# Linear attention over 32 heads: sixteen single warm-up matmuls, a new order for the first heads, and stores spread among the loads

## The chip, the cores and the metric

The kernel runs on one core of one Trainium2 chip. The metric is device time in microseconds (us); lower is better. Five engines run their own instruction lists at the same time: TensorE (PE, matmuls, with PEld for its weight loads), VectorE (DVE), ScalarE (ACT), GpSimd (POOL) and SyncE (SP, which here only issues DMAs). Sixteen DMA engines move the data between memory (HBM) and the core's buffer.

## What is computed

For each of 32 heads, with sequence length S = 2048 and head size D = 128, all in bf16:

```python
phi_q = jnp.where(q > 0, q + 1, jnp.exp(q)) + 1e-6
phi_k = jnp.where(k > 0, k + 1, jnp.exp(k)) + 1e-6
kv = jnp.einsum("bhsd,bhse->bhde", phi_k, v)
z = jnp.einsum("bhsd->bhd", phi_k)
num = jnp.einsum("bhqd,bhde->bhqe", phi_q, kv)
den = jnp.einsum("bhqd,bhd->bhq", phi_q, z)[..., None] + 1e-6
return num / den
```

Each head reads q, k and v (512 KB each) and writes 512 KB. The kernel splits phi(x) into min(exp(x), 1) + 1e-6 and max(x, 0), keeps the two parts apart, and lets TensorE add their products.

## The kernel before

A head is one tile of 128 partitions by 16 blocks of 128 rows. The work of head h is a set of named operations, and every operation is added once in `head(h)`:

- `ldk`, `ldq`, `ldv` (L347): loads of 512 KB into one of NI = 7 buffers each. All are issued by SP, except `ldv0.0`, which ACT issues. A load of head h waits until head h - 7 has been read.
- `ek` (L360, ACT): exp of k; `em` (L363, DVE): min with 1 and add 1e-6, in place. `rkp` (L370, POOL) and, for the first half of head 0 only, `rkd` (L366, DVE): max(k, 0). `v1` (L374, POOL): a copy of v beside a column of ones (`v1ones`, L324). The results of `em`, `rkp` and `v1` have two buffers each, freed by `kv` of two heads before.
- `kv` (L381, PE): 32 matmuls of 129 columns into one PSUM bank that holds both kv and z. `kvs` (L386, DVE): its copy to bf16.
- `T` (L393, PE): 16 transposes of q into PSUM, one buffer only: `T` of the next head waits for `eq` (L397, ACT, exp), `rqa` (L403, ACT, relu of the first half) and `rqb` (L406, DVE, the same for the second half). `emq` (L399, DVE): min with 1 and add 1e-6.
- `n.0` and `n.1` (L417 to L424, PE): the product of phi(q) with kv, 129 columns, in two groups: blocks 0 to 11 in PSUM banks 0 to 3, blocks 12 to 15 in banks 4 and 5. Then on DVE `a` (L437, adds 1e-6 for the second group), `r` (L440, reciprocal) and `f` (L444, the product with the reciprocal, to one of NO = 12 output buffers). `a.1` of head h waits for `kv` of head h + 2, because they share bank 5.
- `st` (L452, SP): the store of a head, 512 KB; the last head is stored in three pieces.
- `w` (L326 to L335, PE): warm-up matmuls of 480 columns on the identity matrix, into a PSUM bank that is not yet in use. They wait for nothing but the identity matrix, so each runs when TensorE's list reaches it.

There is no planner in the kernel: the table `ORDER` (L96) writes out the order of operations on each of the five engines by hand, and every engine runs its list strictly in that order. `Program.resolve` (L194) puts a semaphore wait before an operation for what it needs from another engine. SP's list is one queue: a store that waits for its `f` holds up all loads behind it. `WARM` (L13) gives the number of matmuls in `w0`, `w1`, `w2`.

The loads of heads 1 to 31 are shaped so that memory is read in 32 rows of 16 KB; a store writes 128 rows of 4 KB. SP issues far ahead: a load lands about 18 us after its issue.

Of the kernel before, what the change touches and what calls it, by code (L numbers as in the profile page):

```python
# [94 lines left out]

ORDER = {  # L96
    "PE": """
        w2 w1 T0.0 T0.1 w0 T1.0 kv0.0 kv0.1 n0.0 kv1.0 T2.0 n0.1 kv2.0 n1.0 n1.1 T3.0 kv3.0 n2.0 T4.0 n2.1 kv4.0
        n3.0 T5.0 n3.1 kv5.0 n4.0 T6.0 n4.1 kv6.0 n5.0 T7.0 n5.1 kv7.0 n6.0 T8.0 n6.1 kv8.0 n7.0 T9.0 n7.1 kv9.0
        n8.0 T10.0 n8.1 kv10.0 n9.0 T11.0 n9.1 kv11.0 n10.0 T12.0 n10.1 kv12.0 n11.0 T13.0 n11.1 kv13.0 n12.0  # L100
        T14.0 n12.1 kv14.0 n13.0 T15.0 n13.1 kv15.0 n14.0 T16.0 n14.1 kv16.0 n15.0 T17.0 n15.1 kv17.0 n16.0
        T18.0 n16.1 kv18.0 n17.0 T19.0 n17.1 kv19.0 n18.0 T20.0 n18.1 kv20.0 n19.0 T21.0 n19.1 kv21.0 n20.0
        T22.0 n20.1 kv22.0 n21.0 T23.0 n21.1 kv23.0 n22.0 T24.0 n22.1 kv24.0 n23.0 T25.0 n23.1 kv25.0 n24.0
        T26.0 n24.1 kv26.0 n25.0 T27.0 n25.1 kv27.0 n26.0 T28.0 n26.1 kv28.0 n27.0 T29.0 n27.1 kv29.0 n28.0
        T30.0 n28.1 kv30.0 n29.0 T31.0 T31.1 n29.1 kv31.0 n30.0 n30.1 n31.0 n31.1 n31.2
    """,
    "DVE": """
        eps0 ones emq0.0 em0.0 em0.1 rqb0.0 rkd0.0 v1ones0 v1ones1 eps1 emq0.1 em1.0 eps2 kvs0 emq1.0 r0.0
        rqb1.0 em2.0 kvs1 f0.0 em3.0 a0.1 r0.1 kvs2 f0.1 rqb2.0 r1.0 f1.0 emq2.0 em4.0 a1.1 r1.1 rqb3.0 f1.1
        r2.0 kvs3 f2.0 emq3.0 em5.0 a2.1 r2.1 rqb4.0 f2.1 r3.0 kvs4 f3.0 emq4.0 em6.0 a3.1 r3.1 rqb5.0 f3.1 r4.0  # L110
        kvs5 f4.0 emq5.0 em7.0 a4.1 r4.1 rqb6.0 f4.1 r5.0 kvs6 f5.0 emq6.0 em8.0 a5.1 r5.1 rqb7.0 f5.1 r6.0 kvs7
        f6.0 emq7.0 em9.0 a6.1 r6.1 rqb8.0 f6.1 r7.0 kvs8 f7.0 emq8.0 em10.0 a7.1 r7.1 rqb9.0 f7.1 r8.0 kvs9
        f8.0 emq9.0 em11.0 a8.1 r8.1 rqb10.0 f8.1 r9.0 kvs10 f9.0 emq10.0 em12.0 a9.1 r9.1 rqb11.0 f9.1 r10.0
        kvs11 f10.0 emq11.0 em13.0 a10.1 r10.1 rqb12.0 f10.1 r11.0 kvs12 f11.0 emq12.0 em14.0 a11.1 r11.1
        rqb13.0 f11.1 r12.0 kvs13 f12.0 emq13.0 em15.0 a12.1 r12.1 rqb14.0 f12.1 r13.0 kvs14 f13.0 emq14.0
        em16.0 a13.1 r13.1 rqb15.0 f13.1 r14.0 kvs15 f14.0 emq15.0 em17.0 a14.1 r14.1 rqb16.0 f14.1 r15.0 kvs16
        f15.0 emq16.0 em18.0 a15.1 r15.1 rqb17.0 f15.1 r16.0 kvs17 f16.0 emq17.0 em19.0 a16.1 r16.1 rqb18.0
        f16.1 r17.0 kvs18 f17.0 emq18.0 em20.0 a17.1 r17.1 rqb19.0 f17.1 r18.0 kvs19 f18.0 emq19.0 em21.0 a18.1
        r18.1 rqb20.0 f18.1 r19.0 kvs20 f19.0 emq20.0 em22.0 a19.1 r19.1 rqb21.0 f19.1 r20.0 kvs21 f20.0 emq21.0
        em23.0 a20.1 r20.1 rqb22.0 f20.1 r21.0 kvs22 f21.0 emq22.0 em24.0 a21.1 rqb23.0 r21.1 f21.1 r22.0 kvs23  # L120
        f22.0 emq23.0 em25.0 a22.1 r22.1 rqb24.0 f22.1 r23.0 kvs24 f23.0 emq24.0 em26.0 a23.1 r23.1 rqb25.0
        f23.1 r24.0 kvs25 f24.0 emq25.0 em27.0 a24.1 r24.1 rqb26.0 f24.1 r25.0 kvs26 f25.0 emq26.0 em28.0 a25.1
        r25.1 rqb27.0 f25.1 r26.0 kvs27 f26.0 emq27.0 em29.0 a26.1 r26.1 rqb28.0 f26.1 r27.0 kvs28 f27.0 emq28.0
        em30.0 a27.1 r27.1 rqb29.0 f27.1 kvs29 r28.0 emq29.0 f28.0 em31.0 a28.1 kvs30 rqb30.0 r28.1 f28.1 r29.0
        emq30.0 f29.0 emq31.0 emq31.1 a29.1 r29.1 kvs31 f29.1 emq31.2 r30.0 f30.0 a30.1 r30.1 f30.1 r31.0 f31.0
        a31.1 r31.1 r31.2 f31.1 f31.2
    """,
    "ACT": """
        exp ldv0.0 ek0.0 ek0.1 eq0.0 eq0.1 rqa0 ek1.0 eq1.0 ek2.0 rqa1 ek3.0 eq2.0 rqa2 ek4.0 eq3.0 rqa3 ek5.0
        eq4.0 rqa4 ek6.0 eq5.0 rqa5 ek7.0 eq6.0 rqa6 ek8.0 eq7.0 rqa7 ek9.0 eq8.0 rqa8 ek10.0 eq9.0 rqa9 ek11.0  # L130
        eq10.0 rqa10 ek12.0 eq11.0 rqa11 ek13.0 eq12.0 rqa12 ek14.0 eq13.0 rqa13 ek15.0 eq14.0 rqa14 ek16.0
        eq15.0 rqa15 ek17.0 eq16.0 rqa16 ek18.0 eq17.0 rqa17 ek19.0 eq18.0 rqa18 ek20.0 eq19.0 rqa19 ek21.0
# [6 lines left out]
        rkp6.0 v17.0 rkp7.0 rkp8.0 v18.0 rkp9.0 v19.0 rkp10.0 v110.0 v111.0 rkp11.0 v112.0 rkp12.0 v113.0
        rkp13.0 v114.0 rkp14.0 v115.0 rkp15.0 v116.0 rkp16.0 rkp17.0 v117.0 rkp18.0 v118.0 v119.0 rkp19.0 v120.0  # L140
        rkp20.0 rkp21.0 v121.0 rkp22.0 v122.0 rkp23.0 v123.0 rkp24.0 v124.0 rkp25.0 v125.0 v126.0 rkp26.0 v127.0
        rkp27.0 v128.0 rkp28.0 v129.0 rkp29.0 v130.0 rkp30.0 rkp31.0 v131.0
# [355 lines left out]
```

## Time and profile before

| what | value |
|---|---|
| time, median of 3 runs | 169.61 us (169.48 to 169.76) |
| the profiled execution's own time | 170.02 us |
| its span, first to last instruction | 168.6 us |
| busy: PE, DVE, ACT, POOL | 155.6, 153.7, 149.6, 93.4 us |
| moved by DMA | 67.51 MB, mean 400 GB/s over the span |
| HBM read, written | 50.33 MB, 16.78 MB |
| one head on PE in the middle of the run | 4.62 us |
| share of PE in the chain that ended last | 88% |

The profile is of one execution. Times are counted from the start of its span; the execution takes 1.4 us more than the span (170.02 against 168.6). A row of instructions gives when it began, how long it took, and in brackets how long its engine had been idle and what ended that. A row of a window gives, for each engine, how long it was busy in the window, then the granted TensorE clock (1.00 is full), the share of the 16 DMA engines that was busy (it can be a little over 1, since packets overlap) and the rate at which they moved data. A DMA issue has the time of the issue and the time from there to landing, when the last byte has arrived and the semaphore counts it.

### The profile page before, as it was taken

How to read it: one execution, taken by the hardware profiler on the slowest of the kernel's cores; microseconds unless marked ns; L12 is line 12 of the kernel's file. 1: busy time of each engine (PE TensorE's matmuls, PEld its weight loads, DVE VectorE, ACT ScalarE, POOL GpSimd, SP SyncE). 2: the span in 40 equal slices, each digit the busy share in tenths (PEclk: the TensorE clock that was granted, in tenths of full speed). 3: DMA queues.
4: the chain of work that ended last, by engine and by line, in shares of the span. 5: the costliest groups of instructions: out<-in, count | busy, mean ns of one | idle time of the engine just before them, and what ended most of it. 6: DMA issues, size and time to landing. Idle time of an engine off the chain costs nothing.

```text
span 168.6 us, 6160 instructions
## 1 busy us (share of the span) xinstructions
PE 155.6 (92%) x2702; PEld 151.2 (90%) x2702; DVE 153.7 (91%) x300; ACT 149.6 (89%) x102; POOL 93.4 (55%) x71
## 2 busy tenths in 40 slices
...
DMA  5999999999999999999999999999999999999985
GB/s 206 431 420 424 385 431 393 412 412 406 416 400 412 408 404 408 390 436 402 395 429 419 408 421 425 417 389 430 433 406 404 412 445 390 420 417 414 391 326 225
DMA packets 9819, 67.51 MB, mean 400 GB/s; under 512 B 2080, under 2 KB 2464, under 8 KB 6816
## 3 DMA queue, kind: packets, MB, share of 16 engines
...
q8 instruction: 21, 0.34, 0.8%
...
HBM read 50.33 MB, written 16.78 MB: 398 GB/s over the span
## 4 chain that ended last, share of the span: by engine, by line
PE 88%; DVE 6%; DMA 3%; ACT 1%; issue 0%; SPq 0%
PE la L381 35%; PE la L422 18%; PE la L393 17%; PE la L424 17%; DMA la<-in_q_dram 3%; DVE la L444 3%; DVE la L399 1%; DVE la L363 1%; ACT la L397 1%; DVE la L440 1%; PE la L417 0%; DVE la L406 0%; SPq L348 0%; DVE la L386 0%; DVE la L437 0%
## 5 line engine op out<-in xcount | busy, mean ns | idle before, releaser
L444 DVE TENSOR_TENSOR la<-la 128x1536 bf16<-128x1536 f32 (+2 forms) x65 | 77.7, 1197 | 0.2
L370 POOL TENSOR_SCALAR la<-la 128x2048 bf16<-128x2048 bf16 (+1 forms) x32 | 59.7, 1866 | 29.3 <-PE la L381 23.8
L424 PE MATMUL la<-la 128*128 128x129 bf16 x512 | 67.0, 220 | 0.0
L422 PE MATMUL la<-la 128*128 128x129 bf16 x512 | 67.0, 219 | 0.0
L397 ACT ACTIVATE la<-la 128x2048 bf16<-128x2048 bf16 (+2 forms) x35 | 60.2, 1730 | 6.0 <-PE la L393 3.3
L360 ACT ACTIVATE la<-la 128x2048 bf16<-128x2048 bf16 (+1 forms) x33 | 61.3, 1860 | 3.8 <-PE la L381 2.0
L381 PE MATMUL la<-la 128*128 128x129 bf16 x1024 | 64.4, 222 | 0.0
L381 PEld LDWEIGHTS la<-la 128*128 128x128 bf16 x1024 | 60.5, 99 | 0.0
L374 POOL COPY la<-la 128x1024 int32<-128x1024 int32 (+1 forms) x33 | 34.4, 1043 | 29.5 <-PE la L381 25.5
L424 PEld LDWEIGHTS la<-la 128*128 128x128 bf16 x512 | 49.6, 97 | 0.0
L422 PEld LDWEIGHTS la<-la 128*128 128x128 bf16 x512 | 47.9, 97 | 0.2 <-DVE la L444 0.2
L393 PE MATMUL la<-la 128*128 128x128 bf16 x512 | 34.5, 222 | 4.6 <-DVE la L406 4.2
L393 PEld LDWEIGHTS la<-la 128*128 128x128 bf16 x512 | 30.4, 99 | 5.8 <-ACT la L360 4.6
L403 ACT ACTIVATE la<-la 128x1024 bf16<-128x1024 bf16 (+1 forms) x32 | 33.5, 1046 | 0.0
L399 DVE TENSOR_SCALAR la<-la 128x2048 bf16<-128x2048 bf16 (+2 forms) x35 | 25.3, 724 | 7.3 <-ACT la L397 7.3
L363 DVE TENSOR_SCALAR la<-la 128x2048 bf16<-128x2048 bf16 (+1 forms) x33 | 23.9, 726 | 0.0
L417 PE MATMUL la<-la 128*128 128x3 bf16 (+1 forms) x128 | 21.6, 169 | 2.1 <-DVE la L444 1.7
L406 DVE TENSOR_SCALAR la<-la 128x1024 bf16<-128x1024 bf16 x31 | 20.5, 662 | 0.0
L417 PEld LDWEIGHTS la<-la 128*128 128x128 bf16 x128 | 12.5, 98 | 2.4 <-DVE la L444 1.8
L440 DVE RECIPROCAL la<-la 128x12 f32<-128x12 f32 (+2 forms) x65 | 13.0, 201 | 1.1
L386 DVE CAST la<-la 128x129 bf16<-128x129 f32 x32 | 7.8, 243 | 2.6 <-PE la L381 2.6
L329 PE MATMUL la<-la 128*128 128x480 bf16 x14 | 5.2, 546 | 1.5 <-POOL la L314 1.5
...
## 6 DMA issues: line engine op xcount, KB each, us to landing
...
la<-in_v_dram SPq DMA_DIRECT2D x31, 512.0 KB, 18.5
out_dram<-la SPq DMA_DIRECT2D x31, 512.0 KB, 19.1
...
out_dram<-la SPq DMA_DIRECT2D x1, 128.0 KB, 2.8
```

What stands on the lines that cost most here:

```text
L360: add("ACT", f"ek{h}.{i}", lambda e, a=a, b=b: e.activation(em_sb[:, h % NE, a:b], k_sb[:, h % NI, a:b], ACT.Exp), over("ldk", h, ld_parts ...
L370: add("POOL", f"rkp{h}.{i}", lambda e, a=a, b=b: e.tensor_scalar(rk_sb[:, h % NR, a:b], k_sb[:, h % NI, a:b], BIG, 0.0, op0=ALU.min, op1=A ...
L374: add("POOL", f"v1{h}.{i}", lambda e, a=a, b=b: e.tensor_copy(v1_sb[:, h % NV, a:b, 0:D].bitcast(i32), v_sb[:, h % NI, a:b].bitcast(i32)), ...
L381: ins = e.matmul(kv_ps, lhsT=src[:, j], rhs=v1_sb[:, h % NV, j, 0:NC], start=(j + part == 0), stop=(j == NT - 1 and part == 1))
L393: ins = e.transpose(xT[:, j], q_sb[:, h % NI, j], ident[:])
L397: add("ACT", f"eq{h}.{i}", lambda e, a=a, b=b: e.activation(emq_sb[:, h % NQ, a:b], xT[:, a:b], ACT.Exp), over("T", h, t_parts, a, b) + fr ...
L399: add("DVE", f"emq{h}.{i}", lambda e, a=a, b=b: e.tensor_scalar(emq_sb[:, h % NQ, a:b], emq_sb[:, h % NQ, a:b], 1.0, EPS, op0=ALU.min, op1 ...
L403: add("ACT", f"rqa{h}", lambda e: e.activation(rq_sb[:, h % NQ, 0:n], xT[:, 0:n], ACT.Relu), over("T", h, t_parts, 0, n) + freed(NQ, h, (" ...
L417: e.matmul(_ap(o_ps[:, :], o + D, [[NC, m]]), lhsT=ones[:], rhs=epsr[:, 0:m], start=True, stop=False, skip_group_check=True)
L422: e.matmul(to, lhsT=emq_sb[:, h % NQ, t], rhs=kvs_sb[:, h % NK, 0:NC], start=late and c == 0, stop=False, skip_group_check=True)
L424: ins = e.matmul(to, lhsT=rq_sb[:, h % NQ, t], rhs=kvs_sb[:, h % NK, 0:NC], start=False, stop=True, skip_group_check=True)
L444: return e.tensor_tensor(out=_ap(o_sb[:, :, :, :], first(o_sb[:, h % NO, t0, 0:1]) - first(o_sb[:, :, :, :]), [[m * D, nb], [D, m], [1, D] ...
```

## The change

Three parts, all of them in the tables:

1. `WARM` goes from three blocks of 2, 8 and 4 matmuls to sixteen single matmuls (`w0` to `w15`) and one block of 12 (`w16`). Before, `w2` and `w1` (12 matmuls) stand ahead of `T0.0` and `w0` (2) after `T0.1`. After, 18 stand ahead of `T0.0`, 6 between `T0.0` and `T0.1`, 1 ahead of `kv0.0` and 3 ahead of `T1.0`.
2. The first heads are ordered anew. PE: `kv0.0 kv0.1` now come ahead of `T1.0`, then `kv1.0 n0.0 n0.1 T2.0 kv2.0`. ACT: `ek1.0` moves ahead of `eq0.0`, and `eq1.0` behind `ek2.0`. DVE: `rkd0.0 em0.0 em0.1` come first, ahead of `emq0.0`, and so on up to head 4. From head 4 on, PE and DVE follow the same pattern as before up to the last few heads, where `kvs31` now comes after `emq31.2`. POOL runs `rkp` ahead of `v1` in nearly every head; before, the two stood in either order.
3. SP's list is made anew. Before, `st0` stands 30th among the transfers (with `ldv0.0` counted as the second), `st1` 55th, `st2` 56th, and the stores that follow come single or in groups of two or three. After, `st0` stands 24th and the stores up to `st20` come one by one, on average one per 3.4 loads. In both lists the last load is transfer 117, and the 11 stores from `st21` to `st31` follow. The last load is `ldq31` before and `ldv31` after.

The number of loads, stores and computing operations is the same, apart from the 14 more warm-up matmuls.

```diff
-WARM = (2, 8, 4)
+WARM = (1, 1, 1, 1, 1, 1, 1, 1, 1, 1, 1, 1, 1, 1, 1, 1, 12)
...
     "PE": """
-        w2 w1 T0.0 T0.1 w0 T1.0 kv0.0 kv0.1 n0.0 kv1.0 T2.0 n0.1 kv2.0 n1.0 n1.1 T3.0 kv3.0 n2.0 T4.0 n2.1 kv4.0
+        w16 w6 w7 w8 w9 w10 w2 T0.0 w0 w11 w12 w5 w13 w1 T0.1 w14 kv0.0 kv0.1 w3 w15 w4 T1.0 kv1.0 n0.0 n0.1
+        T2.0 kv2.0 n1.0 T3.0 n1.1 kv3.0 n2.0 T4.0 n2.1 kv4.0 n3.0 T5.0 n3.1 kv5.0 n4.0 T6.0 n4.1 kv6.0 n5.0 T7.0
...
     "DVE": """
-        eps0 ones emq0.0 em0.0 em0.1 rqb0.0 rkd0.0 v1ones0 v1ones1 eps1 emq0.1 em1.0 eps2 kvs0 emq1.0 r0.0
-        rqb1.0 em2.0 kvs1 f0.0 em3.0 a0.1 r0.1 kvs2 f0.1 rqb2.0 r1.0 f1.0 emq2.0 em4.0 a1.1 r1.1 rqb3.0 f1.1
+        v1ones0 eps0 v1ones1 ones rkd0.0 em0.0 em0.1 emq0.0 em1.0 eps1 rqb0.0 eps2 emq0.1 kvs0 em2.0 kvs1 rqb1.0
+        r0.0 f0.0 emq1.0 em3.0 a0.1 kvs2 r0.1 rqb2.0 f0.1 r1.0 emq2.0 f1.0 em4.0 a1.1 r1.1 rqb3.0 f1.1 r2.0 kvs3
...
     "ACT": """
-        exp ldv0.0 ek0.0 ek0.1 eq0.0 eq0.1 rqa0 ek1.0 eq1.0 ek2.0 rqa1 ek3.0 eq2.0 rqa2 ek4.0 eq3.0 rqa3 ek5.0
+        exp ldv0.0 ek0.0 ek0.1 ek1.0 eq0.0 eq0.1 rqa0 ek2.0 eq1.0 rqa1 ek3.0 eq2.0 rqa2 ek4.0 eq3.0 rqa3 ek5.0
...
     "POOL": """
-        ident0 ident rkp0.0 rkp1.0 v10.0 v10.1 v11.0 rkp2.0 v12.0 rkp3.0 v13.0 v14.0 rkp4.0 v15.0 rkp5.0 v16.0
+        ident0 ident rkp0.0 rkp1.0 v10.0 v10.1 v11.0 rkp2.0 v12.0 rkp3.0 v13.0 rkp4.0 v14.0 rkp5.0 v15.0 rkp6.0
...
     "SP": """
-        ldk0.0 ldq0.0 ldk1.0 ldk2.0 ldq1.0 ldv1.0 ldk3.0 ldv2.0 ldq2.0 ldq3.0 ldk4.0 ldv3.0 ldv4.0 ldv5.0 ldk5.0
-        ldv6.0 ldq4.0 ldk6.0 ldq5.0 ldk7.0 ldv7.0 ldk8.0 ldk9.0 ldv8.0 ldq6.0 ldq7.0 ldk10.0 ldv9.0 st0.0 ldq8.0
-        ldv10.0 ldv11.0 ldk11.0 ldq9.0 ldq10.0 ldv12.0 ldq11.0 ldk12.0 ldk13.0 ldv13.0 ldq12.0 ldq13.0 ldq14.0
-        ldq15.0 ldv14.0 ldv15.0 ldq16.0 ldk14.0 ldk15.0 ldk16.0 ldv16.0 ldv17.0 ldk17.0 st1.0 st2.0 ldq17.0
+        ldk0.0 ldq0.0 ldk1.0 ldk2.0 ldv1.0 ldq1.0 ldv2.0 ldk3.0 ldq2.0 ldv3.0 ldk4.0 ldq3.0 ldv4.0 ldv5.0 ldq4.0
+        ldk5.0 ldk6.0 ldv6.0 ldq5.0 ldq6.0 ldk7.0 ldk8.0 st0.0 ldv7.0 ldv8.0 ldq7.0 ldk9.0 ldv9.0 st1.0 ldv10.0
+        ldq8.0 ldk10.0 ldq9.0 ldk11.0 st2.0 ldq10.0 ldq11.0 ldv11.0 st3.0 ldk12.0 ldk13.0 ldv12.0 ldq12.0
...
-        ldk29.0 ldq26.0 ldq27.0 ldk30.0 ldv28.0 st14.0 ldv29.0 st15.0 ldq28.0 ldv30.0 ldq29.0 ldk31.0 st16.0
-        ldq30.0 st17.0 st18.0 st19.0 ldv31.0 st20.0 ldq31.0 st21.0 st22.0 st23.0 st24.0 st25.0 st26.0 st27.0
-        st28.0 st29.0 st30.0 st31.0 st31.1 st31.2
+        ldq26.0 ldv27.0 st15.0 ldk28.0 ldv28.0 ldq27.0 st16.0 ldk29.0 ldq28.0 ldv29.0 st17.0 ldq29.0 ldk30.0
+        ldv30.0 st18.0 ldq30.0 ldk31.0 st19.0 ldq31.0 st20.0 ldv31.0 st21.0 st22.0 st23.0 st24.0 st25.0 st26.0
+        st27.0 st28.0 st29.0 st30.0 st31.0 st31.1 st31.2
```

More of the change, by code (lines that the diff above doesn't have):

```diff
@@ L97 @@
     "PE": """
-        w2 w1 T0.0 T0.1 w0 T1.0 kv0.0 kv0.1 n0.0 kv1.0 T2.0 n0.1 kv2.0 n1.0 n1.1 T3.0 kv3.0 n2.0 T4.0 n2.1 kv4.0
[L99 to L102, printed above, removed]
@@ L103 @@
-        T22.0 n20.1 kv22.0 n21.0 T23.0 n21.1 kv23.0 n22.0 T24.0 n22.1 kv24.0 n23.0 T25.0 n23.1 kv25.0 n24.0
-        T26.0 n24.1 kv26.0 n25.0 T27.0 n25.1 kv27.0 n26.0 T28.0 n26.1 kv28.0 n27.0 T29.0 n27.1 kv29.0 n28.0
-        T30.0 n28.1 kv30.0 n29.0 T31.0 T31.1 n29.1 kv31.0 n30.0 n30.1 n31.0 n31.1 n31.2
+        w16 w6 w7 w8 w9 w10 w2 T0.0 w0 w11 w12 w5 w13 w1 T0.1 w14 kv0.0 kv0.1 w3 w15 w4 T1.0 kv1.0 n0.0 n0.1
+        T2.0 kv2.0 n1.0 T3.0 n1.1 kv3.0 n2.0 T4.0 n2.1 kv4.0 n3.0 T5.0 n3.1 kv5.0 n4.0 T6.0 n4.1 kv6.0 n5.0 T7.0
@@ new lines @@
+        n5.1 kv7.0 n6.0 T8.0 n6.1 kv8.0 n7.0 T9.0 n7.1 kv9.0 n8.0 T10.0 n8.1 kv10.0 n9.0 T11.0 n9.1 kv11.0 n10.0
+        T12.0 n10.1 kv12.0 n11.0 T13.0 n11.1 kv13.0 n12.0 T14.0 n12.1 kv14.0 n13.0 T15.0 n13.1 kv15.0 n14.0
+        T16.0 n14.1 kv16.0 n15.0 T17.0 n15.1 kv17.0 n16.0 T18.0 n16.1 kv18.0 n17.0 T19.0 n17.1 kv19.0 n18.0
+        T20.0 n18.1 kv20.0 n19.0 T21.0 n19.1 kv21.0 n20.0 T22.0 n20.1 kv22.0 n21.0 T23.0 n21.1 kv23.0 n22.0
+        T24.0 n22.1 kv24.0 n23.0 T25.0 n23.1 kv25.0 n24.0 T26.0 n24.1 kv26.0 n25.0 T27.0 n25.1 kv27.0 n26.0
@@ L106 @@
+        T28.0 n26.1 kv28.0 n27.0 T29.0 n27.1 kv29.0 n28.0 T30.0 n28.1 kv30.0 n29.0 T31.0 T31.1 n29.1 kv31.0
+        n30.0 n30.1 n31.0 n31.1 n31.2
     """,
     "DVE": """
-        eps0 ones emq0.0 em0.0 em0.1 rqb0.0 rkd0.0 v1ones0 v1ones1 eps1 emq0.1 em1.0 eps2 kvs0 emq1.0 r0.0
-        rqb1.0 em2.0 kvs1 f0.0 em3.0 a0.1 r0.1 kvs2 f0.1 rqb2.0 r1.0 f1.0 emq2.0 em4.0 a1.1 r1.1 rqb3.0 f1.1
-        r2.0 kvs3 f2.0 emq3.0 em5.0 a2.1 r2.1 rqb4.0 f2.1 r3.0 kvs4 f3.0 emq4.0 em6.0 a3.1 r3.1 rqb5.0 f3.1 r4.0
@@ L111 @@
[L111 to L125, printed above, removed]
@@ L126 @@
-        a31.1 r31.1 r31.2 f31.1 f31.2
+        v1ones0 eps0 v1ones1 ones rkd0.0 em0.0 em0.1 emq0.0 em1.0 eps1 rqb0.0 eps2 emq0.1 kvs0 em2.0 kvs1 rqb1.0
+        r0.0 f0.0 emq1.0 em3.0 a0.1 kvs2 r0.1 rqb2.0 f0.1 r1.0 emq2.0 f1.0 em4.0 a1.1 r1.1 rqb3.0 f1.1 r2.0 kvs3
+        f2.0 emq3.0 em5.0 a2.1 r2.1 rqb4.0 f2.1 r3.0 kvs4 f3.0 emq4.0 em6.0 a3.1 r3.1 rqb5.0 f3.1 r4.0 kvs5 f4.0
+        emq5.0 em7.0 a4.1 r4.1 rqb6.0 f4.1 r5.0 kvs6 f5.0 emq6.0 em8.0 a5.1 r5.1 rqb7.0 f5.1 r6.0 kvs7 f6.0
+        emq7.0 em9.0 a6.1 r6.1 rqb8.0 f6.1 r7.0 kvs8 f7.0 emq8.0 em10.0 a7.1 r7.1 rqb9.0 f7.1 r8.0 kvs9 f8.0
@@ new lines @@
+        emq9.0 em11.0 a8.1 r8.1 rqb10.0 f8.1 r9.0 kvs10 f9.0 emq10.0 em12.0 a9.1 r9.1 rqb11.0 f9.1 r10.0 kvs11
+        f10.0 emq11.0 em13.0 a10.1 r10.1 rqb12.0 f10.1 r11.0 kvs12 f11.0 emq12.0 em14.0 a11.1 r11.1 rqb13.0
+        f11.1 r12.0 kvs13 f12.0 emq13.0 em15.0 a12.1 r12.1 rqb14.0 f12.1 r13.0 kvs14 f13.0 emq14.0 em16.0 a13.1
+        r13.1 rqb15.0 f13.1 r14.0 kvs15 f14.0 emq15.0 em17.0 a14.1 r14.1 rqb16.0 f14.1 r15.0 kvs16 f15.0 emq16.0
+        em18.0 a15.1 r15.1 rqb17.0 f15.1 r16.0 kvs17 f16.0 emq17.0 em19.0 a16.1 r16.1 rqb18.0 f16.1 r17.0 kvs18
@@ new lines @@
+        f17.0 emq18.0 em20.0 a17.1 r17.1 rqb19.0 f17.1 r18.0 kvs19 f18.0 emq19.0 em21.0 a18.1 r18.1 rqb20.0
+        f18.1 r19.0 kvs20 f19.0 emq20.0 em22.0 a19.1 r19.1 rqb21.0 f19.1 r20.0 kvs21 f20.0 emq21.0 em23.0 a20.1
+        r20.1 rqb22.0 f20.1 r21.0 kvs22 f21.0 emq22.0 em24.0 a21.1 r21.1 rqb23.0 f21.1 r22.0 kvs23 f22.0 emq23.0
+        em25.0 a22.1 r22.1 rqb24.0 f22.1 r23.0 kvs24 f23.0 emq24.0 em26.0 a23.1 r23.1 rqb25.0 f23.1 r24.0 kvs25
+        f24.0 emq25.0 em27.0 a24.1 r24.1 rqb26.0 f24.1 r25.0 kvs26 f25.0 emq26.0 em28.0 a25.1 r25.1 rqb27.0
@@ L127 @@
+        f25.1 r26.0 kvs27 f26.0 emq27.0 em29.0 a26.1 r26.1 rqb28.0 f26.1 r27.0 kvs28 f27.0 emq28.0 em30.0 a27.1
+        r27.1 rqb29.0 f27.1 r28.0 kvs29 f28.0 emq29.0 em31.0 a28.1 r28.1 rqb30.0 f28.1 r29.0 kvs30 f29.0 emq30.0
+        emq31.0 a29.1 r29.1 emq31.1 f29.1 emq31.2 kvs31 r30.0 f30.0 a30.1 r30.1 f30.1 r31.0 f31.0 a31.1 r31.1
+        r31.2 f31.1 f31.2
     """,
     "ACT": """
-        exp ldv0.0 ek0.0 ek0.1 eq0.0 eq0.1 rqa0 ek1.0 eq1.0 ek2.0 rqa1 ek3.0 eq2.0 rqa2 ek4.0 eq3.0 rqa3 ek5.0
+        exp ldv0.0 ek0.0 ek0.1 ek1.0 eq0.0 eq0.1 rqa0 ek2.0 eq1.0 rqa1 ek3.0 eq2.0 rqa2 ek4.0 eq3.0 rqa3 ek5.0
@@ L137 @@
     "POOL": """
-        ident0 ident rkp0.0 rkp1.0 v10.0 v10.1 v11.0 rkp2.0 v12.0 rkp3.0 v13.0 v14.0 rkp4.0 v15.0 rkp5.0 v16.0
[L139 to L142, printed above, removed]
+        ident0 ident rkp0.0 rkp1.0 v10.0 v10.1 v11.0 rkp2.0 v12.0 rkp3.0 v13.0 rkp4.0 v14.0 rkp5.0 v15.0 rkp6.0
@@ L143 @@
+        v16.0 rkp7.0 v17.0 rkp8.0 v18.0 rkp9.0 v19.0 rkp10.0 v110.0 rkp11.0 v111.0 rkp12.0 v112.0 rkp13.0 v113.0
+        rkp14.0 v114.0 rkp15.0 v115.0 rkp16.0 v116.0 rkp17.0 v117.0 rkp18.0 v118.0 rkp19.0 v119.0 rkp20.0 v120.0
+        rkp21.0 v121.0 rkp22.0 v122.0 rkp23.0 v123.0 rkp24.0 v124.0 rkp25.0 v125.0 rkp26.0 v126.0 rkp27.0 v127.0
+        v128.0 rkp28.0 rkp29.0 v129.0 rkp30.0 v130.0 rkp31.0 v131.0
     """,
     "SP": """
-        ldk0.0 ldq0.0 ldk1.0 ldk2.0 ldq1.0 ldv1.0 ldk3.0 ldv2.0 ldq2.0 ldq3.0 ldk4.0 ldv3.0 ldv4.0 ldv5.0 ldk5.0
@@ L146 @@
-        ldv6.0 ldq4.0 ldk6.0 ldq5.0 ldk7.0 ldv7.0 ldk8.0 ldk9.0 ldv8.0 ldq6.0 ldq7.0 ldk10.0 ldv9.0 st0.0 ldq8.0
-        ldv10.0 ldv11.0 ldk11.0 ldq9.0 ldq10.0 ldv12.0 ldq11.0 ldk12.0 ldk13.0 ldv13.0 ldq12.0 ldq13.0 ldq14.0
-        ldq15.0 ldv14.0 ldv15.0 ldq16.0 ldk14.0 ldk15.0 ldk16.0 ldv16.0 ldv17.0 ldk17.0 st1.0 st2.0 ldq17.0
-        ldq18.0 ldk18.0 ldv18.0 ldk19.0 ldv19.0 ldk20.0 ldq19.0 st3.0 ldv20.0 ldv21.0 st4.0 ldq20.0 ldk21.0
-        ldq21.0 st5.0 ldk22.0 st6.0 ldq22.0 st7.0 st8.0 ldv22.0 ldk23.0 ldk24.0 ldv23.0 ldk25.0 ldv24.0 ldk26.0
```

5 lines of the change are left out of this document (4 added, 1 removed).

## The prediction

> **What bounds the kernel now.** I read the page first, then the windows by stage, then the DMA issues at the end, and the chain of waits last.
>
> From the page (busy rows; then the 40 slices; then the queues):
>
> ```profile
> span 168.6 us, 6160 instructions
> ...
> PE 155.6 (92%) x2702; PEld 151.2 (90%) x2702; DVE 153.7 (91%) x300; ACT 149.6 (89%) x102; POOL 93.4 (55%) x71
> ...
> DMA  5999999999999999999999999999999999999985
> ...
> q8 instruction: 21, 0.34, 0.8%
> ```
>
> PE, DVE, ACT and the DMA engines are all at nine tenths. The chain of waits puts 88% on PE and 3% on DMA, but it follows instructions back from the last one; a DMA engine that is always one transfer behind does not appear in it. So I asked for the windows (busy time of PE, PEld, DVE, ACT, POOL; clock; DMA share; GB/s):
>
> ```profile
> 24.44:73.17 48.73, 48.73 (x883) 48.33 (x880) 48.35 (x95) 48.36 (x32) 31.15 (x22) 1.00 1.01 407
> 79.51:133.21 53.70, 53.70 (x981) 53.70 (x979) 53.29 (x107) 53.36 (x36) 34.38 (x24) 1.00 1.01 415
> 135.82:154.35 18.53, 18.53 (x342) 18.53 (x339) 18.43 (x37) 18.41 (x13) 11.72 (x8) 1.00 1.01 414
> ```
>
> Everything is full at once: PE runs without a gap, and so do the DMA engines. The end decides which of them is last. The last stores (one issue each: st28, st29, st30, the last piece of st31):
>
> ```profile
> L452 SPq DMA_DIRECT2D out_dram<-la x1: 333/333/333, 155.5 to 155.5; - x1
> DMA to landing us min/median/max: 9.3/9.3/9.3
> ...
> L452 SPq DMA_DIRECT2D out_dram<-la x1: 332/332/332, 159.4 to 159.4; - x1
> DMA to landing us min/median/max: 6.6/6.6/6.6
> ...
> L452 SPq DMA_DIRECT2D out_dram<-la x1: 332/332/332, 162.7 to 162.7; - x1
> DMA to landing us min/median/max: 4.5/4.5/4.5
> ...
> L452 SPq DMA_DIRECT2D out_dram<-la x1: 333/333/333, 165.8 to 165.8; - x1
> DMA to landing us min/median/max: 2.8/2.8/2.8
> ```
>
> They are issued 3 to 4 us apart and land at 164.8, 166.0, 167.2 and 168.6, some 1.3 us apart. That is the pace of the stream, not of the computation. By the issue records all 128 transfers of 512 KB land at such steps, from 7.87 us (the 4th) to the end, but for three steps of 2.50, 2.70 and 2.61 us (at 22-24, 77-79, 133-136). At each of these three, the packet records have a 16 KB instruction fetch (queue q8) of 1.08 to 1.09 us on one engine, the 1st, 9th and 17th of 21: I read this as the same engine delayed three times. A transfer lands when its slowest engine is through, so that engine is the bound: **128 transfers plus three fetches, without a pause from 2 us to the end.**
>
> The computation is close behind. The last product ends at 165.8. The last piece's packets began at 166.66 on engines that were free, and would have landed by about 167.6 (packets to 167.1; the last landing came 0.46 after its last packet). So computation alone would end 168.6 - 167.6 = 1.0 us earlier than the stream does.
>
> **Part 1, warm-ups and the first heads.** What is lost today (a window row, and PE's rows):
>
> ```profile
> 12.00:16.00 4.00, 3.69 (x37) 3.72 (x38) 2.17 (x8) 1.88 (x1) 0.80 (x1) 0.57 0.98 397
> ...
> 12.31 1.66 PE L393 MATMUL la<-la 128*128 128x128 bf16 x16 [4.20 <-DVE la L406]
> 13.77 3.04 PE L381 MATMUL la<-la 128*128 128x129 bf16 x32
> ```
>
> After 4.2 us idle the granted clock falls to half: T1 takes 1.46 us up to kv0 where a later T takes 0.89, and kv0 2.85 where a later kv takes 1.81 (chain of waits): 0.57 + 1.04 = 1.6 us.
>
> Added: 14 matmuls of 480 columns. The 12 of before begin 0.40 us apart, the last two, when the clock is full, 0.20. 18 ahead of T0.0 take, at that trace's turn to full clock (5.74), 4.2 + 7.5 x 0.2 = 5.7 us, to 7.3; if the clock opens late, 18 x 0.4 = 7.2, to 8.7. T0.0 began at 6.63, so it is 0.7 to 2.1 later. That costs nothing, since ACT now does ek1.0 first: k1 lands at 7.87, ek1.0 takes 1.92, to 9.86. Then eq0.0 and eq0.1 (1.94, to 11.8), rqa0 (to 12.7). T0.1 must be done by 10.8: 7.3 + 0.45 + 6 x 0.2 + 0.45 = 9.4, or at the late opening about 11.2 (0.4 lost).
>
> kv0 no longer waits for T1. It waits for the v copies, which end at 11.33 as before (POOL's first five steps are unmoved): kv0 ends at 12.5 at full clock, 13.6 at half; today 16.8. On DVE, kvs0 now stands behind emq0.1. That waits for eq0.1 (11.8), and POOL's rkp2, released by kv0's end, may hold it (see the second rival): kvs0 at 13.6 to 15.1, today 16.84. **The computation gets a lead of 1.7 to 3.2 us.** T1 waits for rqb0.0 (after 12.7), behind kv0 and no more ahead of it; kv1 follows kvs0.
>
> [...]
>
> **Part 2, the loads.** Landing depends on the place in SP's list. With today's landing of each place: ldq27 (102nd, was 100th) lands at 135.8, T27 runs now at about 136.5 (T31's 155.0 less 4 x 4.62). ldk30 (109th, was 101st) 144.5, ek30 now 145.2. ldk31 (113th, was 109th) 149.5, ek31 now 149.85. ldv31 (117th, was 115th) 154.35 and 1.04 for its copy, kv31 now 156.22. Up to head 26 the loads leave at least 3.4 us. So the loads leave today's schedule 0.4 to 0.8 us at the end, and **eat all but that of the lead**: kv31 at 155.4 to 155.8, the last product at 165.0 to 165.4, and computation alone would end at 166.8 to 167.2.
>
> Can SP run dry behind a store? st0 waits for f0.1, which ends at 25.2 at the latest; its turn in the stream is at 33.4. st1 (30th) waits for 30.4 at most, its turn is at 41. Later stores have more room. And f12 finds its buffer free, as st0 lands by 34.7. No cost; if a store came over 8 us late, the stream would stop one for one.
>
> **Part 3, the stream.** The number of transfers is the same, and the last 11 are the same stores. Between the 24th (34.71) and the 117th (154.35) lie 93 transfers in both. Steps per transfer today, without the long ones: 1.282 us in 24.44-73.17 (38 transfers, 1 store: 3%), 1.249 in 79.51-133.21 (43, 11 stores: 26%), 1.235 in 135.82-154.35 (15, 7 stores: 47%). Store after store at the end: 1.293. So mixing is faster than either alone, as the GB/s above say too (407, 415, 414). Today the 93 take 119.64, 2.81 of it the two fetches' excess (1.45 + 1.36). After, 20 of the 93 are stores: 21.5%. On the straight line from 3% to 26% a step is 1.282 - 0.033 x 18.5/23 = 1.2555; 93 x 1.2555 + 2.81 = 119.57: **0.1 us** gained. If 26% and 21.5% are as good as each other, 93 x 1.249 + 2.81 = 118.97: **0.7 us**. I take the middle, 0.4. The 28 more PE instructions (matmuls with their weight loads) are 0.5% of 5404; 21 fetches grow by 0.1, none on the last engine.
>
> [...] The trace reached 415 over long stretches at a DMA share of 1.01, and I give the stream no reserve beyond that.
>
> **Sum.** Against the profiled execution: 170.02 - 0.4 = 169.6 (span 168.2). Against the median: 169.61 - 0.4 = **169.2**, own range 168.9 to 169.5. A measurement of this kernel tells about 0.2% (0.34 us) from no change; 169.27 is that line, so the likeliest case lies on it.
>
> **The rivals.**
> - *The computation is the end.* If the slowest engine isn't one and the same, the landings at the end follow the issues: f ends 0.4 to 0.8 earlier plus what the stream gives (0.4): 169.61 - 1.0 = 168.6. For it: PE without a gap. Against: st30 lands 4.5 us after its issue.
> - *DVE is held by POOL.* DVE's SBUF operations wait while POOL works:
>
> ```profile
> 16.90 1.89 POOL L370 TENSOR_SCALAR la<-la 128x2048 bf16<-128x2048 bf16 x1 [4.10 <-PE la L381]
> 17.05 2.28 DVE L399 TENSOR_SCALAR la<-la 128x2048 bf16<-128x2048 bf16 x1
> 22.62 1.53 DVE L363 TENSOR_SCALAR la<-la 128x2048 bf16<-128x2048 bf16 x1
> 32.26 0.68 DVE L399 TENSOR_SCALAR la<-la 128x2048 bf16<-128x2048 bf16 x1
> ```
>
>   2.28 and 1.53 instead of 0.68. From 27 us on, em ends just as kv's end releases POOL, so they miss each other. Now rkp (1.89) comes ahead of v1 (1.04) after each release: a late em pays 0.85 to 1.6. Against: `a` waits for the same kv, so after one hit PE is late too and they part again. It decides once the hits cost more than 1.0 (the distance to the stream) plus 0.4 to 0.8 in the last heads, two hits. With four: 4 x 0.85 - 1.6 = 1.8 slower, **171.4**.
> - *It does not do what it says:* the clock falls all the same. Lead 0.6 instead of 1.7 or more; the stream ends: 169.2 to 169.6.
> - *The mixed pace belongs to late heads, not to mixing:* 169.6.
>
> **How the numbers follow.** Stream with 0.1 to 0.7 gained: 0.55 (of it 0.37 beyond the line). Computation ends, 168.6: 0.14. No warm clock or no mixing gain, about 169.5: 0.16 (0.04 beyond). DVE held, 171.4: 0.15. Faster 0.55, same 0.30, slower 0.15. Range 168.4 to 169.9: it leaves out most of the slower case and the far end of the second.
>
> **What would show it.** T1 at 0.89 us and a clock of 1.00 in 12-16; kvs0 by 15.1; f1.0 before 24.5 (now 25.98); waits of ACT, POOL or PE on loads from about 134 on; steps of 1.25 between 35 and 75 us; last store still landing over 2.5 us after its issue. Wrong, if the DMA share falls below 1 before 150, if em takes 1.5 beyond the first heads, or if the last landings follow the issues.

## The result, and the profile after

The changed kernel takes **169.19 us** (median of 9 runs, 168.90 to 169.36) against 169.75 us for the kernel before in the same comparison (9 runs, 169.48 to 170.08). The ratio is 0.9964, with a 95% interval of 0.9954 to 0.9975. The profiled execution took 169.27 us with a span of 168.0 us.

In the profile after, line numbers from `ORDER` on are one higher (kv is L382, T is L394, f is L445, st is L453). From its page, the busy rows, the DMA slices and the queue of instruction fetches:

```profile
span 168.0 us, 6186 instructions
...
PE 156.5 (93%) x2716; PEld 150.8 (90%) x2716; DVE 151.9 (90%) x300; ACT 149.7 (89%) x102; POOL 93.2 (55%) x71
...
DMA  5999999999999999999999999999999999999985
...
q8 instruction: 21, 0.34, 0.8%
```

Busy shares, DMA slices and fetches are as before. The windows, first over the three long stretches and then over the early gap (PE, PEld, DVE, ACT, POOL; clock; DMA share; GB/s):

```profile
24.44:73.17 48.73, 48.73 (x889) 48.73 (x887) 48.35 (x96) 48.39 (x33) 29.98 (x22) 1.00 1.01 410
79.51:133.21 53.70, 53.70 (x980) 53.70 (x978) 53.29 (x105) 53.33 (x36) 32.53 (x23) 1.00 1.01 417
135.82:154.35 18.53, 18.53 (x338) 18.40 (x336) 17.87 (x37) 16.56 (x11) 9.07 (x7) 1.00 1.01 415
12.00:16.00 4.00, 3.15 (x46) 2.41 (x44) 3.91 (x7) 4.00 (x3) 3.51 (x3) 1.00 0.98 397
```

Two things moved. The rate is higher by 1 to 3 GB/s in each long stretch (before: 407, 415, 414). It is so although these windows lay between the long steps of before, and the second now holds a long step (130.59 to 132.75). And the clock in 12 to 16 us is 1.00 (before: 0.57). In the third stretch ACT now stands idle for 2 us, where before it was nearly full (18.41 of 18.53), and POOL works 9.07 us instead of 11.72. PE's timeline shows what became of the early gap:

```profile
10.86 1.97 PE L382 MATMUL la<-la 128*128 128x129 bf16 x32 [1.37 <-POOL la L375]
...
13.66 1.07 PE L394 MATMUL la<-la 128*128 128x128 bf16 x16 [0.21 <-DVE la L407]
15.36 1.82 PE L382 MATMUL la<-la 128*128 128x129 bf16 x29 [0.63 <-DVE la L387]
```

kv0 waits only for POOL's v copies and runs at full clock (1.97 us in its row, at 1.00; before 3.04). T1 follows it, and kv1 has begun at 15.36, where before kv0 itself was at work up to 16.8. The stores at the end (st28, st29, and the last piece of st31):

```profile
L453 SPq DMA_DIRECT2D out_dram<-la x1: 332/332/332, 154.1 to 154.1; - x1
DMA to landing us min/median/max: 10.1/10.1/10.1
...
L453 SPq DMA_DIRECT2D out_dram<-la x1: 332/332/332, 158.3 to 158.3; - x1
DMA to landing us min/median/max: 7.0/7.0/7.0
...
L453 SPq DMA_DIRECT2D out_dram<-la x1: 332/332/332, 164.7 to 164.7; - x1
DMA to landing us min/median/max: 3.2/3.2/3.2
```

They are issued 1.1 to 1.4 us earlier than before, but wait longer: 3.2 us for the last piece instead of 2.8. The last products on DVE, of before and of after (start, duration):

```profile
164.23 1.55 DVE L444 TENSOR_TENSOR la<-la 128x768 bf16<-128x768 f32 x2
```

```profile
163.16 1.55 DVE L445 TENSOR_TENSOR la<-la 128x768 bf16<-128x768 f32 x2
```

The last product is out at 164.72 (before 165.79), the last landing is at 167.93 (before 168.59). The computation gained 1.07 us, the stream 0.66, and the time followed the stream.

### The profile page after: what moved, and what is told of

Read it like the earlier page. It is cut to its first block, busy times and chain, and to the rows that moved or that the text cites. A ratio compares the mean times of both kernels' runs of the same rounds, so it can differ in the third digit from the quotient of the medians.

```text
span 168.0 us, 6186 instructions
## 1 busy us (share of the span) xinstructions
PE 156.5 (93%) x2716; PEld 150.8 (90%) x2716; DVE 151.9 (90%) x300; ACT 149.7 (89%) x102; POOL 93.2 (55%) x71
## 4 chain that ended last, share of the span: by engine, by line
DVE 74%; PE 15%; DMA 4%; issue 3%; ACT 1%; SPq 0%
DVE la L445 36%; DVE la L400 10%; DVE la L364 10%; DVE la L407 9%; PE la L382 7%; DVE la L441 4%; DMA la<-in_k_dram 4%; DVE la L387 3%; PE la L423 3%; PE la L394 3%; PE la L425 3%; DVE la L438 2%; ACT la L361 1%; ACT la L398 1%; SPq L349 0%
## 5 line engine op out<-in xcount | busy, mean ns | idle before, releaser
L445 DVE TENSOR_TENSOR la<-la 128x1536 bf16<-128x1536 f32 (+2 forms) x65 | 77.7, 1196 | 0.1
L382 PE MATMUL la<-la 128*128 128x129 bf16 x1024 | 63.3, 220 | 2.0 <-POOL la L375 1.4
L382 PEld LDWEIGHTS la<-la 128*128 128x128 bf16 x1024 | 59.3, 98 | 2.5 <-issue 1.7
L394 PE MATMUL la<-la 128*128 128x128 bf16 x512 | 34.0, 219 | 1.3 <-DVE la L387 0.9
L394 PEld LDWEIGHTS la<-la 128*128 128x128 bf16 x512 | 29.9, 98 | 2.7 <-DVE la L387 1.0
L400 DVE TENSOR_SCALAR la<-la 128x2048 bf16<-128x2048 bf16 (+2 forms) x35 | 24.0, 687 | 4.5 <-ACT la L398 4.5
L330 PE MATMUL la<-la 128*128 128x480 bf16 x28 | 7.8, 428 | 1.5 <-POOL la L315 1.5
```

The source lines that it names most:

```text
L382: ins = e.matmul(kv_ps, lhsT=src[:, j], rhs=v1_sb[:, h % NV, j, 0:NC], start=(j + part == 0), stop=(j == NT - 1 and part == 1))
L394: ins = e.transpose(xT[:, j], q_sb[:, h % NI, j], ident[:])
L400: add("DVE", f"emq{h}.{i}", lambda e, a=a, b=b: e.tensor_scalar(emq_sb[:, h % NQ, a:b], emq_sb[:, h % NQ, a:b], 1.0, EPS, op0=ALU.min, op1 ...
L445: return e.tensor_tensor(out=_ap(o_sb[:, :, :, :], first(o_sb[:, h % NO, t0, 0:1]) - first(o_sb[:, :, :, :]), [[m * D, nb], [D, m], [1, D] ...
```

## The experiments

The theory: **the end is the stream's** (128 transfers and the instruction fetches), so the new list of SP gives the gain and the rest of the change gives none. The rivals: the earlier computation gives it; the warm-ups give it; the two lists alone differ, whatever runs beside them. The kernel before was timed again on each chip, beside the kernels that ran there. Its median was 170.08 us beside `e1`, `e2`, `e3`; 170.13 beside `s1` to `s4`; 170.03 beside `a_again`, `e6`, `e7`, `e8`; 169.92 beside `s5`. Every ratio below is against those runs.

### The parts of the change, one at a time

`e1_sp_new`: the kernel before, with the new list of SP alone.

```diff
     "SP": """
-        ldk0.0 ldq0.0 ldk1.0 ldk2.0 ldq1.0 ldv1.0 ldk3.0 ldv2.0 ldq2.0 ldq3.0 ldk4.0 ldv3.0 ldv4.0 ldv5.0 ldk5.0
+        ldk0.0 ldq0.0 ldk1.0 ldk2.0 ldv1.0 ldq1.0 ldv2.0 ldk3.0 ldq2.0 ldv3.0 ldk4.0 ldq3.0 ldv4.0 ldv5.0 ldq4.0
...
```

> The kernel before with only SP's list (loads and stores) from the changed kernel; warm-ups and the other four lists are the old ones. Theory A (the stream of transfers ends the run, and the spread stores make its steps shorter): all of the gain is here, 169.2 where before runs at 169.7, ratio 0.996 to 0.998; the steps between the 24th and the 117th landing shorten by 0.3 to 0.6 us in sum, and the last product still ends near 165.8. Theory B (the computation's lead made the gain): no gain, 169.7, ratio 0.999 to 1.001.

Measured: 169.49 us, and a wide spread, 169.15 to 170.73 in 12 runs; ratio 0.9983 (0.9961 to 1.0004). The interval includes no change, so by itself it does not settle the matter. Eight runs lie between 169.15 and 170.06, four at 170.53 to 170.73. These four have low mean clocks, 0.976 to 0.978, but so has one run at 169.55 (0.976). The profiled execution is one of the four. Its windows around the early gap:

```profile
12.00:16.00 4.00, 3.35 (x32) 3.38 (x33) 2.17 (x8) 1.68 (x2) 0.80 (x1) 0.50 0.98 397
16.00:20.00 4.00, 3.61 (x50) 3.34 (x48) 1.98 (x2) 2.41 (x3) 1.93 (x2) 0.71 1.02 414
```

The clock is at half from 11.52 to 18.34 us, for 6.82 us. In the profile of before it was 3.41 us, 12.57 to 15.98, with about the same idle time of PE (4.25 us here, 4.20 there). The last piece of this execution:

```profile
L452 SPq DMA_DIRECT2D out_dram<-la x1: 332/332/332, 167.3 to 167.3; - x1
DMA to landing us min/median/max: 1.9/1.9/1.9
```

It lands 1.9 us after its issue, the least in any of these profiles: no queue holds it up. So in this execution the computation ended last, with the low clock of the early gap twice as long. That the clock sets apart the other long runs too is likely by their mean clocks, not shown. The median (169.49 against 170.08) moves as the theory has it, the four long runs as the rival has it.

`e2_sp_old`: the changed kernel with the old list of SP, everything else as changed.

```diff
     "SP": """
-        ldk0.0 ldq0.0 ldk1.0 ldk2.0 ldv1.0 ldq1.0 ldv2.0 ldk3.0 ldq2.0 ldv3.0 ldk4.0 ldq3.0 ldv4.0 ldv5.0 ldq4.0
+        ldk0.0 ldq0.0 ldk1.0 ldk2.0 ldq1.0 ldv1.0 ldk3.0 ldv2.0 ldq2.0 ldq3.0 ldk4.0 ldv3.0 ldv4.0 ldv5.0 ldk5.0
...
```

> The changed kernel with SP's old list; the warm-ups and the four other lists are the new ones. Theory A: no gain, 169.7, ratio 0.999 to 1.001, though the computation has its lead of 2 us over the first heads. Theory B: the gain is here, 169.2, ratio 0.996 to 0.997.

Measured: 170.69 us, ratio 1.0035 (1.0023 to 1.0047): **slower than before**. The last product came at 167.66 and the last piece landed 1.86 us after its issue, so the computation ended this one. The place is in the last heads. POOL's rows, then DVE's, of this kernel (start, duration):

```profile
136.22 1.04 POOL L375 COPY la<-la 128x1024 int32<-128x1024 int32 x1 [3.93 <-DMA la<-in_v_dram]
137.22 4.19 POOL L371 TENSOR_SCALAR la<-la 128x2048 bf16<-128x2048 bf16 x2
```

```profile
137.81 1.86 DVE L400 TENSOR_SCALAR la<-la 128x2048 bf16<-128x2048 bf16 x1
139.59 2.37 DVE L364 TENSOR_SCALAR la<-la 128x2048 bf16<-128x2048 bf16 x1
```

With the old list v28 lands at 136.10 us (133.85 in the changed kernel), and `v128` stands ahead of `rkp28` on POOL's list. So POOL idles 3.9 us and then runs two `rkp` one after the other, just where DVE's `emq` and `em` come. They take 1.86 and 2.37 us instead of 0.68 and 0.69. In the kernel before v28 lands as late (135.82), but its computation is later as well: POOL waits 2.5 us, and `emq` beside it takes 0.84. `e7_pool_swap` changes that one place in `e2_sp_old`:

```diff
-        v128.0 rkp28.0 rkp29.0 v129.0 rkp30.0 v130.0 rkp31.0 v131.0
+        rkp28.0 v128.0 rkp29.0 v129.0 rkp30.0 v130.0 rkp31.0 v131.0
```

> The changed kernel with SP's old list, as before, and with rkp28 ahead of v128 on POOL. With v128 first, POOL waited 3.9 us for v28 and then ran rkp28 and rkp29 back to back, and DVE's emq and em beside them took 1.86 and 2.37 us instead of 0.68. If these held operations made that kernel slower than before (1.0035): they go back to 0.7 to 1.0, the last product ends 1.5 to 2.5 us earlier, and the ratio falls to 0.997 to 1.000, what the old list's stream gives. If the late loads themselves made it slow: 1.002 to 1.004 as it was.

Measured: 169.90 us, ratio 0.9990 (0.9982 to 0.9999). The same two instructions on DVE:

```profile
137.78 0.68 DVE L400 TENSOR_SCALAR la<-la 128x2048 bf16<-128x2048 bf16 x1
138.38 0.69 DVE L364 TENSOR_SCALAR la<-la 128x2048 bf16<-128x2048 bf16 x1
```

The hold is gone, the last product comes 1.4 us earlier than in `e2` (166.29; 1.5 to 2.5 was expected), and the last piece lands 2.2 us after its issue. The old list with the new computation is back within 0.1% of the kernel before. Its last product is later than that of before (165.79): here too the lead of the first heads does not last to the end.

`e3_old_warm`: the changed kernel with the three old blocks of warm-ups, and none after `w0`.

```diff
-WARM = (1, 1, 1, 1, 1, 1, 1, 1, 1, 1, 1, 1, 1, 1, 1, 1, 12)
+WARM = (2, 8, 4)
...
-        w16 w6 w7 w8 w9 w10 w2 T0.0 w0 w11 w12 w5 w13 w1 T0.1 w14 kv0.0 kv0.1 w3 w15 w4 T1.0 kv1.0 n0.0 n0.1
+        w2 w1 T0.0 T0.1 w0 kv0.0 kv0.1 T1.0 kv1.0 n0.0 n0.1
```

> The changed kernel with the old warm-ups: 12 ahead of T0.0, 2 behind T0.1, none in the gaps; all else new. Theory A: the same time as the changed kernel, 169.2, ratio 0.996 to 0.997, whether the clock falls or not. Theory B (the gaps' warm-ups hold the clock, and this is the gain): the clock falls to half at about 12.6 us, kv0 to kv1 take some 1.5 us more, and the time goes back to 169.7.

Measured: 169.17 us (168.95 to 169.21), ratio 0.9941 (0.9929 to 0.9952). That is the changed kernel's time. In its profile the clock is 1.00 from 5.49 us until after the last product, without the added warm-ups: with kv0 ahead of T1, PE's longest idle time in the early gap is 2.4 us instead of 4.2.

```profile
12.00:16.00 4.00, 2.55 (x42) 2.20 (x40) 3.91 (x7) 4.00 (x3) 3.30 (x3) 1.00 0.97 393
```

That is one execution. The mean clocks of its five runs are 0.977 to 0.994; those of the changed kernel's 15 runs (in the comparison at the start and in `a_again`) are 0.991 to 1.000. An estimate: a mean of 0.977 or 0.982 over 167.8 us is 7.7 or 6.0 us of half clock, and from the end of PE's last matmul (162.87 in the profile) to the end of the span there are only 5.0. So without the added warm-ups the clock fell in three of the five runs before PE was done, most likely in the early gap. The time did not follow: the run at 0.977 is the fastest of the five (168.95).

`a_again` is the changed kernel, once more, beside the three that follow.

> The changed kernel as it is, timed again beside the next three on one chip. All theories: ratio 0.994 to 0.997, all runs within 0.3 us of each other.

Measured: 169.16 us (168.98 to 169.31), ratio 0.9948 (0.9934 to 0.9962).

`e6_warm_gap` is the kernel before with 22 warm-ups in the gap behind T0.1; `e8_sp_new_warm` is that and the new list of SP.

```diff
-WARM = (2, 8, 4)
+WARM = (22, 8, 4)
```

> The kernel before with 22 instead of 2 warm-ups behind T0.1 (4.4 us at full clock, in the gap of 4.8 us ahead of T1.0), and nothing else. Theory C (before, the stream and the computation end together, and the computation is up to 1.5 us later when the clock falls): the low clock goes from the records (0.99 and up), the last product ends 1 to 1.6 us earlier, and the time falls by 0.1 to 0.4 us to what the old list's stream gives, ratio 0.998 to 0.9995. Theory A (the stream alone ends the run of before): the same time, ratio 0.9995 to 1.0005. Theory B (computation alone): 1.6 us less, ratio 0.991.

> The same 22 warm-ups with SP's new list; the heads' old order on the other engines. Theory C: with the clock held the computation is never last, the runs at 170.1 to 170.7 that the new list alone had are gone, all runs lie at 169.0 to 169.5, ratio as of the changed kernel, 0.994 to 0.997. If the late runs of the new list alone had another cause than the clock: they stay.

Measured: 169.82 us for `e6`, ratio 0.9991 (0.9981 to 1.0001); 169.30 us for `e8`, ratio 0.9955 (0.9942 to 0.9969), range 169.13 to 169.37. The warm-ups held the clock in the gap (1.00 in 8 to 20 us), and `e8` has none of the long runs of `e1`; with five runs that can be chance, if one in three is long. In `e6` the last product came at 166.47, later than in the kernel before (165.79), though f0 began 1.5 us earlier: from kvs26 to kvs27 it took 1.8 us longer than the usual 4.62. v28 came late again (POOL waits 3.7 us for it), and `emq` and `em` were held as in `e2`:

```profile
137.66 1.66 DVE L399 TENSOR_SCALAR la<-la 128x2048 bf16<-128x2048 bf16 x1
139.24 1.52 DVE L363 TENSOR_SCALAR la<-la 128x2048 bf16<-128x2048 bf16 x1
```

So the lead that was expected at the end did not come. In `e8` one `emq` is held too (1.66 us at 142.04). In the profiles of both kernels the last piece lands 1.9 us after its issue, so the computation ended them by a little, against what was expected of `e8`.

What these nine profiles say together. The store `st29` lands behind its queue in each of them (4.2 us or more after its issue, where `st30` needs 3.65 in the runs that the computation ended) and marks the stream alone. With the old list it lands at 166.06 (before), 166.05 (`e2`), 165.81 (`e6`) and 165.97 (`e7`); with the new list at 165.37 (after), 165.33 (`a_again`), 165.27 (`e1`), 165.26 (`e3`) and 165.21 (`e8`). No two overlap; the means differ by **0.69 us**. With one and the same list, the order of the first heads and the warm-ups move it by 0.25 us at most. In times, on one chip: 169.90 to 169.16 (`e7` to `a_again`, which differ in SP's list and in the one swap on POOL: 0.74) and 169.82 to 169.30 (`e6` to `e8`, SP's list alone: 0.52). In the profiles of the second pair the gain comes by way of the computation, which gets v28 earlier (133.94 instead of 135.76). On that chip the whole change is worth 0.87 (170.03 to 169.16), so the rest of it gives 0.13 (170.03 to `e7`).

### The stream by itself

`s1_old`, `s2_new`, `s3_apart`: only the transfers of the kernel, with no computation; a store writes a constant, and waits for no product. `s1` has the old order, `s2` the new one, `s3` all loads and then all stores.

```diff
+            for i in range(NO):
+                nc.vector.memset(o_sb[:, i], 1.0).then_inc(made, 1)
...
+            if op.startswith("ld"):
+                load(nc.sync, op[2], h)
...
+                nc.sync.dma_start(rows(of, h)[:, a:b], o_sb[:, h % NO, a:b]).then_inc(get(name), 16)
```

> Only the transfers, in the old order of SP's list: the same loads and stores, no computation (it stores a constant instead of the result), and hardly any instructions to fetch. Theory A (the run is as long as its stream: 128 transfers and three instruction fetches on one engine): the before's 169.7 less the fetches' excess of 1.2 + 1.4 + 1.4 = 4.0 us, 165 to 166, with steps of 1.25 to 1.28 and no long steps. Theory B (the computation ends the run): clearly shorter than that, under 163.

> Only the transfers, in the new order; no computation, a constant is stored. If mixing as such makes the steps shorter: 0.3 to 0.7 us less than the old order alone. If the gain needs the computation: the same time as the old order alone.

> Only the transfers, all 96 loads first and then all stores; no computation, a constant is stored. If the step depends on the mix (1.282 with loads alone, 1.25 mixed): 96 x 1.28 + 32 x 1.29, about 1.5 us more than the new order alone. If it does not: the same time.

Measured: 167.34 us (167.12 to 167.64), 167.15 (167.00 to 167.20) and 167.90 (167.72 to 168.10). Mixing is worth 0.56 to 0.75 us against loads and stores apart, half of the 1.5 that was expected. Between the two mixtures, 0.19 us: the intervals of their ratios overlap (0.9823 to 0.9852, 0.9809 to 0.9838), and from the 24th to the 117th landing they take 118.03 and 117.97 us (the profile of `s1` is of its fastest run). So **the rival that the lists differ by themselves is not borne out**: by themselves they differ by 0.19 us or less, and most of the 0.69 needs something beside the stream.

The page of `s2` begins:

```profile
span 165.8 us, 176 instructions
```

It has no row of queue q8, which has the 21 fetches of the kernels with PE. `s4_new_pe` puts 2716 matmuls of 128 columns beside the same stream, as many as the changed kernel has, with no other computation; `s5_new_pe2` puts 5432 of 32 columns.

```diff
-PE_N, PE_COLS = 0, 128
+PE_N, PE_COLS = 2716, 128
```

> The transfers in the new order and, beside them, 2716 matmuls of 128 columns with their weight loads on TensorE that nothing waits for; no computation of the result. If the long steps come from TensorE's instruction fetches: about 21 fetches of 16 KB again, three long steps in the landings, and 3 to 4.5 us more than the new order alone. If they come from elsewhere: the same time as the new order alone.

> The transfers in the new order and 5432 matmuls of 32 columns beside them, twice the instructions of the run with 2716 and about the same time on TensorE; no computation of the result. That run was 2.25 us longer than the transfers alone, with 21 fetches. If each fetch costs the stream its share: 42 fetches, five or six long steps, 4 to 5 us more than the transfers alone, 171 to 172. If it is TensorE's work beside the stream and not its fetches: 169.4 as with 2716.

Measured for `s4`: 169.40 us (169.33 to 169.60), ratio to before 0.9959 (0.9944 to 0.9974). From its page:

```profile
span 168.1 us, 5608 instructions
...
q8 instruction: 21, 0.34, 0.8%
```

The 21 fetches are back, and with them three long steps of 2.44, 2.56 and 2.65 us among the landings. The last landing is at 167.86 us against 165.53 in `s2`. `s4` takes 2.25 us more than `s2`, less than the 3 to 4.5 expected, and as long as the changed kernel within 0.25 us (169.40 against 169.16 to 169.19). From the 24th to the 117th landing it takes 119.11 us, the changed kernel 119.16 and 118.97. **The changed kernel is as long as its transfers with PE's instructions beside them; there is no sign that ACT, DVE, POOL or a wait adds to it.** No run puts PE's instructions beside the old order.

`s5` was to take 171 to 172 us. It took 225.3, since PE itself needed 223 us for its instructions, so its time says nothing. Its stream says more: 27 fetches had begun before the last landing, there were four long steps (2.82, 2.99, 2.93, 2.67), and the last landing was at 169.81, which is 4.28 after that of `s2`. More instructions with shorter matmuls cost the stream more, which speaks for the fetches and against the matmuls' own work. Per long step that is 2.33 / 3 = 0.8 us in `s4` and 4.28 / 4 = 1.1 us in `s5`.

## Why the prediction was right, point by point

- **The number: right.** The time is 169.19 us, where 169.2 was forecast. The gain is 0.56, where 0.4 was: the kernel before takes 169.75 in this comparison, and 169.61 in the runs that the prediction had.
- **The bound: right.** The stream ends the changed kernel in its profile. The last landing is 3.2 us after its issue, st28 to st30 land 1.2 us apart, and `s4` without any other computation is as long.
- **The distance of 1.0 us between computation and stream: right for the profiled execution only.** In the profile of `e1`, with twice the time at half clock, kvs0 came at 18.02 instead of 16.84 and the last product at 167.29 instead of 165.79, and the computation ended it. Four of its 12 runs were as long. The prediction knew the clock of one execution. Its 1.0 itself fits: with the 1.9 us of a last piece that no queue holds up, the computation of before would have ended at 167.7, 0.9 ahead of the stream.
- **Part 1: right in its steps.** T0.0 began at 7.01 (7.3 predicted), kvs0 at 15.02 (13.6 to 15.1), T1 took 1.07 us in its row (before 1.66; a later T takes 1.06). The lead was 1.6 us (f1.0) to 1.8 us (kvs0), at the low end of 1.7 to 3.2. That it is worth next to nothing by itself was right as well: `e7` against before, 0.9990 (0.9982 to 0.9999). The clock was 1.00 in 12 to 16 us, as forecast, but the single warm-ups were not needed for it in the profile of `e3`, where the order (kv0 ahead of T1) was enough. By the mean clocks they may hold it in more of the runs; the time is the same with and without them.
- **Part 2: right, with a term a little small.** Loads eat part of the lead: from 134 us on POOL waits 2.2 to 2.9 us at a time for v28, k30, k31 and v31. The last product came at 164.72, against 165.0 to 165.4 predicted: the loads left 1.07 us of the lead, not 0.4 to 0.8. No store came so late that SP ran dry: by issues and landings, at least 8 transfers were under way at any time from 10 to 140 us.
- **Part 3: the size right, by luck; the reason not.** The 93 transfers from the 24th to the 117th take 119.32 to 119.65 us in the four profiles with the old list, and 118.97 to 119.16 in the five with the new one, a difference of 0.44 between the means, where 0.4 was forecast (0.1 to 0.7). But steps of 1.25 us were to appear between 35 and 73 us, and they are 1.275 there (30 steps in 38.26 us; before 1.282). The share of stores does not set the pace by itself: `s1` and `s2` differ by 0.06 us over the same 93. And 0.25 of the 0.69 at `st29` lie outside the 93, where nothing was forecast. So the rule that gave 0.4 (steps by the share of stores, and the middle of two readings) is not what made the gain.
- **Fetches: the reading borne out as far as it can be seen, the size too high.** In `s1` to `s3`, where PE does nothing, queue q8 is empty and the longest step between landings is 1.91 us; in `s4` there are three long ones, which end 2 to 3 us after the 1st, 9th and 17th fetch began. The trace keeps the 16 arrivals that make up a landing. At the three long steps of before, 15 have come by 23.21, 78.18 and 134.44, and the last comes 1.2 to 1.4 us later (24.44, 79.51, 135.82): one sixteenth of the transfer is late. That it is the same engine each time is not shown, since the records do not name it. Costed at their step's excess of 1.2 to 1.45 us, three are 4 us, and `s1` was expected at 165 to 166 us by that; it took 167.34, and `s4` against `s2` gives 2.33. Part of the excess is made up again: without the two long steps' excess, the 93 transfers take 116.4 us in `s4` and 117.97 in `s2`.
- **The rival "DVE is held by POOL": did not happen in the changed kernel beyond the first heads** (from 16 us on the worst `emq` there takes 1.11 us, the worst `em` 0.69), **but it is real.** `e2` has it, ends slower than before, and `e7` takes it away; `e6` has it too. It needed only two held instructions, as the prediction had worked out. What it had not seen is what sets it off: computation that is early, a v that is late, and `v1` ahead of `rkp` on POOL's list. In the changed kernel v28 lands 2.3 us earlier than in `e2`.
- **"The computation is the end"** holds in the profiles of `e2` and `e1`, and by a hair in those of `e6` and `e8`, whose last pieces land 1.9 us after their issue; not in the changed kernel.

**What stays open:** why the two orders differ by 0.4 us over 93 transfers when PE's fetches and the computation run beside them, and by 0.06 when they do not. The sum of the long steps' excess (steps over 1.6 us among the 93, less 1.25 each) doesn't explain it: 2.75 to 3.04 us with the old list, 2.47 to 3.17 with the new. The typical step does differ: the median of the 93 is 1.266 to 1.267 us in the four profiles with the old list and 1.246 to 1.248 in the five with the new one and in `s4`, but 1.280 in `s1` and 1.274 in `s2`. So in these runs the shorter step comes only with the new order and PE's instructions together; why, no run shows. The old order with PE's instructions alone was not tried, nor a list with the old share of stores but the new order of loads.
